# Gate and up of a fused FNet and ReGLU layer: one pass over all tokens with 33 block products in place of two passes with 18

## The chip, the cores and the metric

The kernel runs on 1 core of a Trainium2 chip. The metric is the device time of one execution in microseconds (us), the median of several runs; smaller is better. The core has five engines that work side by side and wait for each other by semaphores: PE (matmul, into the PSUM memory), DVE (elementwise), ACT (elementwise and functions), POOL or GpSimd (elementwise here, and issue of transfers), and SP (issue of transfers). SBUF is the memory on the chip from which they work. An engine takes its instructions in order.

## The reference

```python
xn = layernorm(x)                                   # x: 1 x 2048 x 640
a, b = xn @ hid_re.T, xn @ hid_im.T                 # 640 x 640
y = seq_re @ a - seq_im @ b                         # 2048 x 2048
gate, up = xn @ W_gate, xn @ W_up                   # 640 x 1728
h = gate * (gate > 0) * up
out = x + y + h @ W_down                            # 1728 x 640
```

All in float32. The 2048 tokens and 640 features are the sizes that set the work; 1728 is 13 times 128 plus 64.

## The kernel before

Float32 accuracy is had by splitting each operand into a high part in the rounded format fp32r and a low part that is the rest. One *product* is a 128x128 weight block by a 128x512 token block, and `mm3` makes it of three matmuls (high by high, high by low, low by high), L139 to L141. To split, ACT writes the high part (`copy`, L130, or the first line of `split`, L133) and DVE subtracts it (L134, L875).

The work runs in three stages.

**Stage one** normalizes the tokens and applies the sequence transform. It streams the transform matrices (`raw`, `tk`) in, splits them into a ring of buffers (`cb`) and multiplies by the tokens (`xs_early`, `xs_late`). It goes chunk by chunk of 512 columns; a scheduler sets the order of its instructions from the order in which `drive(4, 2)` starts units. The results are added on DVE to `sa` and `sb` and stored to DRAM as `pq` (L667). Beside it, `token_sets` makes sums and differences of token blocks for the second stage, on DVE, and stores them to DRAM (`sets`).

**Stage two, gate and up,** covers 398.2 to 730.4 us. A weight tile of 128 columns of gate and of up holds 10 blocks of 128x128. The tokens are taken in two halves `q` of 1024, and the loop `gate_up(n)` runs 26 units: 13 weight tiles for each half. In a unit, a 2x2 block scheme with fewer products (sums `S1` to `S4` of weights and `T1` to `T4` of tokens) makes 18 products in place of 20. So a weight tile costs 36 products. `Weights` loads a tile (640 KB) for each unit, makes its sums on DVE (`sums`, L861 to L865) and splits them. Partial results are copied from PSUM by ACT (`p`, `u`, L130) and added on DVE (L945, L963); `finals` makes relu(gate) times up (L888) and POOL stores 512 KB of `hd` (L889). The 64 leftover columns of gate and up go through `gate_up_rest`, 10 products for each half, at the start and at the end of the stage; their weights are `wr`. Also in this stage, `pair_weights` and `quad_weights` prepare sums of the last stage's weights (`pw`) and store them in DRAM (`wparts`, `wquads`), and `grow` adds up parts of `hd` and `pq` by transfers (`grown`).

The order in stage two is written by hand: PE, DVE and ACT (`PINNED`) take their instructions as the Python code calls them; the order of SP's and POOL's transfers is left to the scheduler.

**Stage three, the last stage,** from 730.4 us, multiplies hidden rows by the down weights and the hidden transform. It loads token rows (`rw`, from `pq` and `hd`) and weights (`wt`, from `wparts`) through SP, splits the rows into `cb` and multiplies. Its order comes from `drive_last`, which starts after named instructions of stage two (`issue_after`). Its first unit, the *lead*, was prepared in stage two by `lead_load` and `lead_split`; its 18 matmuls stand between the last product of stage two and the others of stage three.

```python
        for f in urgent[n]:
            f()
        copy(p1, b1)
        if ahead:
            ahead.high(0)
        block(b2, A12, B21, True, False)
        block4(b2, A4, 0, True)
        tt(oa[:, c0], b2, p1, op=OP.add)
        if n > 0:
            the_rest()
        if n + 2 < NU:
            weights[n + 2] = Weights(n + 2)
```

## Time and profile before

| what | value |
|---|---|
| median of 3 runs | 1023.11 us (1022.81 to 1023.18) |
| span of the profiled execution, first to last instruction | 1021.1 us |
| instructions in it | 12761 |
| HBM read and written | 203.26 and 72.89 MB |
| busy share of the span: PE, weight loads, DVE, ACT, POOL | 99, 82, 81, 45, 11% |
| gate and up in the trace | 398.2 to 730.4 us |

The time of the profiled execution itself is known by its span only. In the views, an instruction is named by its engine, its line in the kernel, what it writes and what it reads (`out<-in`), with the tile's partitions and elements. A group's row gives the busy time of all, the mean duration of one in ns, and the idle time of the engine just ahead of them with what ended it. A row of the timeline gives the start and the duration in us, then the instruction, then in brackets the idle time before and its releaser. A row of a window gives its length and the busy time of each engine. "PE 99%" in the chain of work means that, followed back from the last instruction, 99% of the span was PE's own.

### The profile page before, as it was taken

How to read it: one execution, taken by the hardware profiler on the slowest of the kernel's cores; microseconds unless marked ns; L12 is line 12 of the kernel's file. 1: busy time of each engine (PE TensorE's matmuls, PEld its weight loads, DVE VectorE, ACT ScalarE, POOL GpSimd, SP SyncE). 2: the span in 40 equal slices, each digit the busy share in tenths (PEclk: the TensorE clock that was granted, in tenths of full speed). 3: DMA queues.
4: the chain of work that ended last, by engine and by line, in shares of the span. 5: the costliest groups of instructions: out<-in, count | busy, mean ns of one | idle time of the engine just before them, and what ended most of it. 6: DMA issues, size and time to landing. Idle time of an engine off the chain costs nothing.

```text
span 1021.1 us, 12761 instructions
## 1 busy us (share of the span) xinstructions
PE 1015.6 (99%) x4510; PEld 840.8 (82%) x4510; DVE 823.5 (81%) x1162; ACT 454.9 (45%) x588; POOL 117.2 (11%) x189
## 2 busy tenths in 40 slices
PE   9999999999999999999999999999999999999998
PEld 7888888888888888888888888888888888888887
DVE  7967976969979697688888977787597888589887
ACT  6664453333334444434445444443443454454552
POOL 2000010121110001321111111111100000000001
PEclk9999999999999999999999999999999999999999
DMA  9884744976869666874658989899798879999784
GB/s 336 314 270 173 265 149 142 330 259 200 348 210 340 222 190 224 261 232 167 232 208 286 285 295 316 289 341 313 234 335 250 256 249 325 328 326 315 219 284 165
DMA packets 113872, 267.57 MB, mean 262 GB/s; under 512 B 13104, under 2 KB 58096, under 8 KB 112176
## 3 DMA queue, kind: packets, MB, share of 16 engines
q1 hardware_dynamic: 92416, 179.03, 52.5%
q0 software_dynamic: 20960, 87.31, 24.6%
q8 instruction: 35, 0.57, 0.2%
q10 hardware_dynamic: 432, 0.43, 0.1%
q14 instruction: 29, 0.24, 0.1%
HBM read 203.26 MB, written 72.89 MB: 270 GB/s over the span
## 4 chain that ended last, share of the span: by engine, by line
PE 99%; DMA 0%; ACT 0%; DVE 0%; SPq 0%; issue 0%
PE ps L140 32%; PE ps L139 32%; PE ps L141 32%; PE ps L527 3%; PE ps L556 1%; PE ps L1368 1%; DMA raw<-in_dft 0%; ACT cb L357 0%; ACT xs_early L258 0%; DVE y L1225 0%; SPq L596 0%; ACT mv L234 0%
## 5 line engine op out<-in xcount | busy, mean ns | idle before, releaser
L139 PE MATMUL ps<-cb,wt 128*128 128x512 f32 (+1 forms) x407 | 157.9, 388 | 0.0
L141 PE MATMUL ps<-cb,wt 128*128 128x512 f32 (+1 forms) x407 | 157.9, 388 | 0.0
L140 PE MATMUL ps<-cb,wt 128*128 128x512 f32 (+1 forms) x407 | 157.9, 388 | 0.0
L133 ACT ACTIVATE cb<-rw 128x1024 fp32r<-128x1024 f32 (+1 forms) x94 | 89.2, 960 | 77.1 <-PE ps L141 56.5
L134 DVE TENSOR_TENSOR cb<-rw,cb 128x1024 fp32r<-128x1024 f32 (+1 forms) x94 | 102.6, 1101 | 22.3 <-ACT cb L133 21.7
L133 ACT ACTIVATE cb<-raw 128x1024 fp32r<-128x1024 f32 x64 | 67.9, 1061 | 105.2 <-PE ps L141 97.0
L134 DVE TENSOR_TENSOR cb<-raw,cb 128x1024 fp32r<-128x1024 f32 x64 | 78.2, 1222 | 31.5 <-ACT cb L133 31.3
L141 PE MATMUL ps<-xs_early,gw 128*128 128x512 f32 x260 | 101.2, 389 | 0.0
L139 PE MATMUL ps<-xs_early,gw 128*128 128x512 f32 x260 | 101.2, 389 | 0.0
L140 PE MATMUL ps<-xs_early,gw 128*128 128x512 f32 x260 | 101.1, 389 | 0.0
L139 PE MATMUL ps<-cb,xs_late 128*128 128x512 f32 x232 | 90.2, 389 | 0.0
L140 PE MATMUL ps<-cb,xs_late 128*128 128x512 f32 x232 | 90.2, 389 | 0.0
L141 PE MATMUL ps<-cb,xs_late 128*128 128x512 f32 x232 | 90.2, 389 | 0.0
L139 PEld LDWEIGHTS ps<-cb,wt 128*128 128x128 f32 x407 | 76.4, 188 | 16.0 <-DVE y L1225 0.2
L141 PEld LDWEIGHTS ps<-cb,wt 128*128 128x128 f32 x407 | 76.4, 188 | 15.7
L140 PEld LDWEIGHTS ps<-cb,wt 128*128 128x128 f32 x407 | 76.4, 188 | 15.6
L139 PE MATMUL ps<-cb,xs_early 128*128 128x512 f32 x226 | 87.9, 389 | 0.0
L140 PE MATMUL ps<-cb,xs_early 128*128 128x512 f32 x226 | 87.9, 389 | 0.0
L141 PE MATMUL ps<-cb,xs_early 128*128 128x512 f32 x226 | 87.9, 389 | 0.0
L130 ACT ACTIVATE gw<-z 128x1024 fp32r<-128x1024 f32 (+1 forms) x52 | 56.4, 1110 | 38.6 <-PE ps L141 23.6
L130 ACT ACTIVATE u<-ps 128x512 f32<-128x512 f32 x52 | 31.1, 598 | 89.6 <-PE ps L141 77.7
L875 DVE TENSOR_TENSOR gw<-z,gw 128x1024 fp32r<-128x1024 f32 (+1 forms) x52 | 64.8, 1284 | 1.9 <-ACT gw L130 1.8
(209 smaller groups left out, 1989.4 us busy)
## 6 DMA issues: line engine op xcount, KB each, us to landing
raw<-in_dft SPq DMA_DIRECT2D x94, 512.0 KB, 5.4
wt<-wparts SPq DMA_DIRECT2D x74, 256.0 KB, 4.3
wparts<-pw POOLq DMA_DIRECT2D x12, 1408.0 KB, 7.9
z<-in_wgu SPq DMA_DIRECT2D x26, 640.0 KB, 5.6
rw<-hd SPq DMA_DIRECT2D x27, 512.0 KB, 6.2
hd<-ob POOLq DMA_DIRECT2D x26, 512.0 KB, 4.8
wt<-wparts SPq DMA_DIRECT2D x29, 384.0 KB, 5.4
rw<-pq SPq DMA_DIRECT2D x19, 512.0 KB, 6.4
```

The lines of the kernel that those rows point to most:

```text
L130: return nc.scalar.activation(o, i, AF.Copy)
L133: nc.scalar.activation(hi, src, AF.Copy)
L134: return nc.vector.tensor_tensor(lo, src, hi.bitcast(F32), op=OP.subtract)
L139: nc.tensor.matmul(ps, wh, mh, start=first, stop=False, skip_group_check=more)
L140: nc.tensor.matmul(ps, wh, ml, start=False, stop=False, skip_group_check=more)
L141: nc.tensor.matmul(ps, wl, mh, start=False, stop=last, skip_group_check=more)
L527: nc.tensor.matmul(E[0, key], xn_part(n * SG + j, d)[v == 1], b[:, int(v == 2), j], start=False, stop=n % NH == NH - 1 and (j, v) == (SG - ...
L556: nc.tensor.matmul(E[c, key], xn_part(j, d)[v == 1], b[c][0][:, int(v == 2), j], start=j == 0 and v == 0, stop=False)
L875: tt(self.w[:, 1, cs], self.z[:, cs], self.w[:, 0, cs].bitcast(F32), op=OP.subtract)
L1368: nc.tensor.matmul(B[out], w[:, v, oo : oo + P], b, start=False, stop=last and v == 1, skip_group_check=more)
```

## The change

Gate and up now goes once over all 2048 tokens. The 5 blocks of each weight (gate and up) and 4 chunks of 512 tokens form a 2x5 by 5x4 block product that is made by 33 products for a weight tile in place of 36. Each product takes a weight operand (raw or one of 23 sums) and a token operand (raw or one of 28 sums and differences). The results share partial sums that live in PSUM:

- `seed` copies a bank of PSUM to another, with a sign, and the next products add to it (ACT, L940); `snap` copies a bank to SBUF (`ev`, ACT, L175); `add` adds a snap into a bank, `addout` and `both` make sums, `final` makes relu(gate) times up (DVE, L950 to L967). A weight tile has 8 seeds, 9 snaps, 4 adds, 7 addouts, 1 both and 4 finals.
- Tables give each step of a weight tile a key, in units of one product. The steps of neighbouring tiles lie 33 keys apart and overlap; all events of the stage are sorted by key, and PE, DVE and ACT take them in that order.
- Weights are loaded once (13 times 640 KB). Their sums are made by GpSimd, 23 of 128x128 a tile (L907), and split by ACT and DVE in pieces (`w3` of 3 blocks, `w1`, `wa`, `wb`).
- The token sums are made by GpSimd in stage one, in 4 slices of 128 columns a chunk (`token_slice`, 10 operations of 128x512 and 41 of 128x128 each), and kept in DRAM (`tok`). 18 raw blocks are loaded and split at the end of stage one; the 28 sums are loaded and split in stage two, 14 of them into the pool `mv` and 14 into slots of `xs_early` and `r1` that come free.
- The leftover columns' 20 products stand at the start: 10 ahead of the first tile, 10 in the gaps of the first tile. The lead's 6 products stand in the gaps of the last tile.
- Results are stored by SP, 52 times 256 KB (L970). The preparation for the last stage comes as 29 tasks (24 `pair_half`, 5 quads) at even distances; all of `grown` is made in stage two.

By the two orders, PE has 4377 matmuls after and 4494 before, and POOL has 221 transfers after and 166 before.

```diff
-        def sums(self):
-            a21, z = self.z2[:, : 2 * P], self.z
-            zz = lambda b: z[:, b : b + 2 * P]
-            tt(zz(S1), a21, zz(A22), op=OP.add)
-            tt(zz(S2), zz(S1), zz(A11), op=OP.subtract)
...
+STEPS = (
+    (0.0, 'mm', 11, 0, 0, 20, 'new', -1), (1.59, 'seed', 16, 11, -1, ()), (3.0, 'mm', 16, 0, 1, 21, '', -1),
+    (4.0, 'mm', 13, 0, 2, 18, '', 11), (5.59, 'seed', 19, 13, 1, ()), (6.5, 'seed', 20, 16, 1, ()),
...
+    (46.6, 'both', 7, 10, 25, -1, 1, ()), (48.0, 'mm', 7, 6, 1, 44, '', -1), (49.59, 'addout', 7, 17, '-', (7,)),
...
+    (62.0, 'mm', 3, 7, 0, 47, '', 10), (64.44, 'addout', 3, 9, '-', (3,)), (65.6, 'final', 3, 7, ()),
+)
...
+        def sums(part):
+            for o, op, a, b in part:
+                pin(tt(at(o), at(a), at(b), op=OP.add if op == "+" else OP.subtract))
...
+    for n, b in (("mv", UPPER), ("prep", 2), ("w3", 5), ("w1", 3), ("wa", 2), ("wb", 2), ("ev", 11)):
...
+    def sum_step(n, o, op, a, b):
+        nc.gpsimd.tensor_tensor(operand(n, o), operand(n, a), operand(n, b), op=OP.add if op == "+" else OP.subtract)
...
+    def seed(n, x, s, sign, done):
+        banks[n, x] = new_bank()
+        nc.scalar.activation(banks[n, x], banks[n, s], AF.Copy, scale=float(sign))
+        release(n, done)
...
+    def add_snap(n, x, s, op, done):
+        b = banks[n, x]
+        tt(b, b, snaps[n, s], op=OP.add if op == "+" else OP.subtract)
+        release(n, done)
...
+        held["dve"] = nc.vector.scalar_tensor_tensor(t, i0, 0.0, i1, op0=OP.max, op1=OP.mult)
+        release(n, done)
+        cs = slice(g % 2 * CH, (g % 2 + 1) * CH)
+        nc.sync.dma_start(hd[g // 2][TILES[n]][:, cs], t)
...
+    for i, o in enumerate(combos[:UPPER]):
+        at(-59, load_upper, o)
+        at(-5 + 1.35 * i, split_slot, o)
...
+    for i, (load, prepare, rounded, store) in enumerate(tasks):
+        key = first_task + (last_task - first_task) * i / (len(tasks) - 1)
+        at(key - 14, load)
+        at(key, prepare)
+        at(key + SPLIT_AHEAD, rounded)
+        at(key + SPLIT_AHEAD + 2, store)
...
+    for i in range(3):
+        for j in range(SG):
+            at(END + (36, 37, 40, 41, 44, 45)[2 * i + j] + 0.3, lead_multiply, i, j)
+
+    events.sort(key=lambda e: e[:2])
     with tc.manual_schedule(engines=PINNED):
-        third[0]()
...
+        for key, _, f in events:
             f()
```

The first place is ACT's row at the start of gate and up, in the new program. `w3` and `w1` are rounded weights, `mv` token sums, `ev` copies out of PSUM, `ps` to `ps` is a seed; the brackets name the queues and engines waited for (DMASW: transfers issued by POOL, DMAHW: by SP).

```order
L178 ACTIVATE pw_3328<-st_3326 128x640
L175 ACTIVATE w3_3381<-gw_3359 128x384 [waits DMASW4_49,DMASW5_49,DMASW3_49,DMASW6_49,DMASW2_49,DMASW7_49,DVE_49,Pool_49]
L175 ACTIVATE w1_3386<-gw_3359 128x128
L178 ACTIVATE mv_3331<-mv_3331 128x512 [waits DMAHW4_49,PE_49,Activation_49]
L1002 ACTIVATE ev_3415<-ps_3316 64x512 [waits PE_49]
L178 ACTIVATE mv_3333<-mv_3333 128x512 [waits DMAHW5_49]
L175 ACTIVATE w3_3429<-gw_3359 128x384 [waits Pool_49]
L178 ACTIVATE mv_3335<-mv_3335 128x512 [waits DMAHW6_49]
L178 ACTIVATE mv_3337<-mv_3337 128x512 [waits DMAHW7_49]
L793 ACTIVATE mv_3339<-mv_3339 128x512 [waits DMAHW0_49]
L1002 ACTIVATE ev_3456<-ps_3317 64x512 [waits PE_49]
L940 ACTIVATE ps_3320<-ps_3318 128x512 [waits PE_49]
```

Before, the weights were rounded into buffers of their own; now the first `w3` waits for six queues of POOL, the last of them that of the last store of `sa`, since the memory of `w3` held `sa` and `sb`. The third seed follows 9 rows further on.

The second place is SP's row at the hand-over to the last stage. Before (L855 is the load of the last unit's weights, `rw` and `wt` belong to the last stage):

```order
L855 DMA z_5477<-in_wgu 128x1280 [waits DMAHW7_49,DVE_49]
L1289 DMA wt_5805<-wparts_94 128x2x384 [waits DMAHW0_49,PE_49]
L1261 DMA rw_5807<-pq2_88 128x1024 [waits DMAHW1_49,DMASW3_49,DVE_49]
L1261 DMA rw_5809<-pq2_88 128x1024 [waits DMAHW2_49,DVE_49]
L1289 DMA wt_5811<-wparts_94 128x384 [waits DMAHW3_49]
```

After (L970 are the stores of finals; the last four of them are shown):

```order
L970 DMA hd1_90<-ev_6570 128x512 [waits DMAHW5_49,DVE_49]
L1308 DMA wt_6738<-wparts_93 128x2x384 [waits DMAHW6_49,PE_49]
L970 DMA hd0_89<-ev_6646 128x512 [waits DMAHW7_49,DVE_49]
L970 DMA hd0_89<-ev_6586 128x512 [waits DMAHW0_49,DVE_49]
L1280 DMA rw_6740<-pq2_87 128x1024 [waits DMAHW1_49]
L970 DMA hd1_90<-ev_6681 128x512 [waits DMAHW2_49,DVE_49]
L1280 DMA rw_6742<-pq2_87 128x1024 [waits DMAHW3_49]
```

The loads of the last stage stood behind a weight load of stage two, and now stand behind and between stores that wait for DVE's last finals.

The third place is PE's row there, in the new program: the end of gate and up and the first product of the last stage.

```order
L186 MATMUL ps_3316<-mv_6485,mv_6487 128x512
L184 MATMUL ps_3319<-xs_early_75,wb_6503 128x512 [waits Activation_49]
...
L184 MATMUL ps_3318<-xs_early_75,w3_6606 128x512 [waits DVE_49]
...
L186 MATMUL ps_3320<-r1_2858,wb_6503 128x512
L184 MATMUL ps_3322<-r1_2858,w1_6351 128x512
L185 MATMUL ps_3322<-r1_2858,w1_6351 128x512
L186 MATMUL ps_3322<-r1_2858,w1_6351 128x512
L184 MATMUL ps_3321<-cb_6752,wt_6738 128x512 [waits Activation_49]
L185 MATMUL ps_3321<-cb_6752,wt_6738 128x512 [waits DVE_49]
```

The lead products (`mv_6485` by `mv_6487`) now stand ahead of the last five products of gate and up, and the last stage's `cb` follows these directly; before, the 18 lead matmuls stood in between.

663 lines of the change are left out of this document (309 added, 354 removed), and 32 rows, old and new, of tables (STEPS, SUMS, TOKEN_SUMS, WEIGHTS).

## The prediction

> **What bounds the kernel now.** I read the page's shares and its chain of work first.
>
> ```profile
> span 1021.1 us, 12761 instructions
> ...
> PE 1015.6 (99%) x4510; PEld 840.8 (82%) x4510; DVE 823.5 (81%) x1162; ACT 454.9 (45%) x588; POOL 117.2 (11%) x189
> ...
> PEclk9999999999999999999999999999999999999999
> ...
> PE 99%; DMA 0%; ACT 0%; DVE 0%; SPq 0%; issue 0%
> ```
>
> TensorE (PE) is busy 99% of the span, it is 99% of the chain, and its granted clock reads 9 in each slice. No wait of another engine sets the end, so the span is the number of matmuls times their spacing. Next come the windows of gate and up (405.0 to 723.4, its 26 units) and of one chunk of the sequence transform (columns: busy time of PE, weight loads, DVE, ACT, POOL; clock; DMA share; GB/s).
>
> ```profile
> 405.00:723.40 318.40, 318.40 (x1406) 263.55 (x1405) 252.99 (x438) 137.76 (x185) 57.71 (x92) 1.00 0.81 270
> 202.00:268.00 66.00, 66.00 (x293) 54.66 (x292) 55.13 (x64) 22.45 (x22) 11.59 (x17) 1.00 0.76 273
> ```
>
> PE has no idle time in either. A matmul costs 318.40/1406 = 0.2265 us, a product of three 0.680 us. DVE is 79% busy in gate and up, ACT 43%.
>
> **What the change removes.** 13 weight tiles lose 3 of 36 products: 13 × 3 × 3 = 117 matmuls, 117 × 0.2265 = **26.5 us**. The 20 products of the 64 leftover columns and the 6 lead products stay and only move. Since PE is the bound with nothing beside it, all 26.5 us would be gained if PE stayed fed. The sum below is therefore 26.5 us less the new stalls of PE.
>
> **Can the others keep up in one tile's 33 products (33 × 0.680 = 22.4 us)?** The rows for the prices:
>
> ```profile
> L963 DVE TENSOR_TENSOR oa<-ps,u 128x512 f32<-128x512 f32 x26 | 17.9, 690 | 34.6 <-PE ps L141 34.6
> L862 DVE TENSOR_TENSOR z<-z 128x256 f32<-128x256 f32 x26 | 11.1, 425 | 0.9
> L865 DVE TENSOR_TENSOR z<-z 128x128 f32<-128x128 f32 x26 | 7.4, 284 | 0.0
> L133 ACT ACTIVATE cb<-raw 128x1024 fp32r<-128x1024 f32 x64 | 67.9, 1061 | 105.2 <-PE ps L141 97.0 <-issue 5.0 <-DVE st L447 1.7
> L130 ACT ACTIVATE u<-ps 128x512 f32<-128x512 f32 x52 | 31.1, 598 | 89.6 <-PE ps L141 77.7 <-DVE sets_b L440 5.5 <-DVE sets_b L421 5.5
> L360 POOL TENSOR_TENSOR cb<-raw,cb 128x512 fp32r<-128x512 f32 x3 | 3.8, 1289 | 0.0
> ...
> 7.44 0.19 POOL L364 TENSOR_TENSOR mv<-stat,cb 128x1 f32<-128x1 f32 x1 [6.99 <-DVE cb L360]
> ...
> 610.20 0.69 DVE L963 TENSOR_TENSOR oa<-ps,u 128x512 f32<-128x512 f32 x1 [1.73 <-PE ps L141]
> 610.81 0.41 DVE L1050 TENSOR_TENSOR pw<-pw 128x256 f32<-128x256 f32 x1
> ```
>
> The last two rows show that a DVE instruction starts 0.08 us before its forerunner's recorded end, so a 128x512 takes 0.61 us of DVE. DVE has 16 such steps on PSUM in a tile (4 add, 7 addout, 1 both, 4 final): 9.8 us. The low halves of the weights are 8 of 128x384 (about 0.48 us of DVE, between the rows of 256 and 512 columns less the same 0.08), one of 512 and one of 128 columns (0.61 and 0.20): 4.6 us. Preparing the last stage's weights adds 29 tasks over 13 tiles, each four 128x128 sums and a low half, 1.3 us: 2.9 us a tile. That makes 17.3 us of 22.4, 77%, as now. ACT has 8 seeds and 9 snaps (0.598 us recorded, 0.52 with the same overlap): 8.8 us, some 4 us of high halves and 1 us of preparation: 14 us, 62%. GpSimd has 23 sums of 128x128, which no row shows: bounds 0.19 us (one column) and 1.29 us (512 columns); on the line between them 0.46 us, 10.7 us a tile, 48%. At the upper bound 23 × 1.29 = 29.7 us would exceed the tile, and GpSimd would be the bound; I take 0.46 since the one-column row shows the fixed part. DVE writing PSUM and ACT copying PSUM to PSUM have no row either: 0.60 to 0.69 us is what the same sizes cost from PSUM to SBUF, and I use that; if PSUM output cost the 128x1024 row's 1.06 us, ACT's 8 seeds would add 3.7 us a tile and still fit. So nothing is over 100%; what is lost, is lost to lateness at single places.
>
> **Place 1, the start of gate and up.** Now:
>
> ```profile
> 398.40 0.39 PE L139 MATMUL ps<-xs_early,wr 128*128 128x512 f32 x1
> ...
> 398.99 0.68 DVE L566 TENSOR_TENSOR sa<-ps,sa 128x512 f32<-128x512 f32 x1
> ...
> 400.07 0.53 POOL L667 DMA_DIRECT2D pq<-sa  x1 [7.54 <-DVE z L861]
> 404.60 1.09 POOL L417 DMA_DIRECT2D sets_b<-rows  x2 [4.00 <-DMA pq<-sa]
> ```
>
> The last sums of the transform are stored at 400.07 and their memory is free at 404.60. In the new order ACT's first weight rounding (w3) waits for that very store, and in ACT's row stand 19 more activations behind it up to the third seed. The 10 leftover products last from 398.4 to 405.2. After 404.6 ACT does w3, w1 and the first token split (0.48 + 0.25 + 0.52 us, the first two estimated on the line between ACT's rows), so the first product starts at 405.9 instead of 405.2, and it waits for DVE's low half of the token block, 0.4 us more. The first seed is ACT's eighth after that, ready near 405.9 + 8 × 0.52 = 410.1; its product has three products ahead of it and could start at 408.3: 1.8 us. By the same count the next two seeds come 0.9 and 0.3 us late, and the one behind them about 1. That is 5 us in the first 12 products. To product 60 DVE has 28 token splits beside the tile work (17.3 − 2.9 = 14.4 us a tile, 26.2 in 60 products): 28 × 0.61 + 26.2 = 43.3 us in 60 × 0.68 = 40.8 us, 2.5 us more. Value **7.5 us**; bounds 0 (if memory is free and the loads are early) and 12.
>
> **Place 2, the hand-over to the last stage.** Now:
>
> ```profile
> 713.23 1.26 SPq L1289 DMA_DIRECT2D wt<-wparts  x1
> 714.53 0.47 SPq L1263 DMA_DIRECT2D rw<-hd  x1
> ...
> 731.27 0.36 SPq L1263 DMA_DIRECT2D rw<-hd  x1
> ...
> 731.04 2.52 ACT L133 ACTIVATE cb<-rw 128x1024 fp32r<-128x1024 f32 x3
> ...
> 732.12 2.96 DVE L134 TENSOR_TENSOR cb<-rw,cb 128x1024 fp32r<-128x1024 f32 x3 [0.27 <-ACT cb L133]
> ...
> rw<-pq SPq DMA_DIRECT2D x19, 512.0 KB, 6.4
> ...
> st<-pq SPq DMA_DIRECT2D x1, 512.0 KB, 3.6
> ...
> L134 DVE TENSOR_TENSOR cb<-raw,cb 128x1024 fp32r<-128x1024 f32 x64 | 78.2, 1222 | 31.5 <-ACT cb L133 31.3
> ```
>
> The last stage's raw blocks are issued on SP before 715.11, and 18 lead matmuls (4.1 us) run while they are rounded from 731.0 on. In the new order the stores of the results stand on SP, and the first raw block (rw) stands behind the stores of finals 0 and 1 of the last tile. These finals wait for the last products: after PE's last product DVE still has addout 4, final 0 and final 1, some 1.5 us, SP's waiting stores take 0.5 us more, so rw is issued 2 us after PE's last product, lands 3.6 to 6.4 us later, is rounded by ACT (1.06 us) and, before the second matmul, by DVE (1.22 us). The lead products have by then gone into the gaps of the last tile and cover nothing. PE waits 2 + 3.6 + 2.3 = 8 to 2 + 6.4 + 2.3 = 11 us. Value **9 us**; bounds 0 (issued as early as now) and 11. A place further on is not late again: the loads behind are issued within 2 us.
>
> **Between them.** The tables leave little room at three places of a tile: the sum `both 7` is asked for at 13.6 products and needed by a product at 15 (0.95 us, for a 0.69 us step); add 23 to seed 1 to its product, 0.3 us spare; seed 16, 0.4 us. One of 29 preparation tasks (four 128x128 sums, over 1 us in one burst) comes every 12 products; I take one in two to strike such a place, some 12 to 14 strikes of 0.4 us: **5 us**, bounds 0 and 10. PE is in order, so each is lost.
>
> **What costs nothing.**
>
> ```profile
> z<-in_wgu SPq DMA_DIRECT2D x26, 640.0 KB, 5.6
> ```
>
> Token sums on GpSimd in the first stage: 4 slices of 41 × 0.46 + 10 × 1.29 = 32 us, 127 us in a first stage of 398 us, beside a busy PE; if they are late, tokens come late and place 1 grows. DVE loses its token work there, which gains nothing while PE is full. The weights are loaded 13 times 640 KB in place of 26, the stores carry the same bytes, and the DMA share was 0.81 with PE full; so I take nothing for transfers, and what a late queue costs stands under D.
>
> **The sum.** −26.5 + 7.5 + 5 + 9 = −5.0 us against the profiled 1021.1: 1016.1. The median of the runs is 1023.11, 2.0 us above the span, so **1018.1 us**. With the bounds of the three places (0 to 33 us) and 26.5 off: 996.6 to 1029.6.
>
> **Rivals.** (B) The cover is better: loads and rounding are early, hand-over 3, start 3, between 1 us. Time 1023.1 − 26.5 + 7 = 1003.6. For it: ACT's and DVE's shares leave a quarter free. Against it: the orders of both places, as told.
> (C) Slower: DVE and GpSimd get in each other's way at SBUF. Rows that bear on it:
>
> ```profile
> 7.59 1.29 POOL L360 TENSOR_TENSOR cb<-raw,cb 128x512 fp32r<-128x512 f32 x1
> ...
> 4.87 0.42 DVE L251 TENSOR_SCALAR r<-r,mv 128x384 f32<-128x384 f32 x1
> ...
> 8.43 0.66 DVE L251 TENSOR_SCALAR r<-r,mv 128x384 f32<-128x384 f32 x1
> ```
>
> The same DVE operation takes 0.42 us with GpSimd idle and 0.66 us when it starts inside a GpSimd sum (7.59 to 8.88). Some 24 DVE steps of each tile read SBUF with both inputs (weight lows, finals, preparation, and split lows), 312 in all, and a GpSimd sum runs for 48% of the time. If each that meets one waits 0.23 us, half a sum, that is 312 × 0.48 × 0.23 = 34 us of DVE, and GpSimd waits as long. DVE would rise from 77% to near 90% of a tile; with the narrow places I take half to reach PE, 17 us, from 12 to 25 with a first stage that suffers too. Time 1018 + 18 = 1036, 1030 to 1043. It decides from about 5 us of lost PE time on. Against it: the first stage's DVE has slack, and a late step costs nothing outside the three narrow places.
> The Trainium skill, "SBUF — State Buffer", section "Who interferes with whom", says that DVE and GpSimd share a port pair as an exclusive lock, held for a whole instruction, and that a DVE instruction with two SBUF inputs competes for it with a GpSimd one that reads SBUF. The stretch from 0.42 to 0.66 us agrees in kind; no DVE row with two SBUF inputs meets a GpSimd sum in this trace, so the rule stays open here. By it the sum would be 1036, without it 1018.
> (D) GpSimd's queue is late as a whole: its sums, the preparation's stores and the growing of hd stand in one row, and a sum that waits holds all behind it. A weight sum late by a quarter of a tile (5.6 us) in half of the tiles costs 36 us: 1054. For it: one in-order queue with 299 sums and 221 DMAs (166 before). Against it: 48%, and sums asked for 10 to 40 products ahead.
> That the change does not do what it says I leave out: the new program's PE row has 117 matmuls fewer.
>
> **Chances.** Forecast (1009 to 1025) 0.40; B (997 to 1009) 0.17; C 0.33; D 0.10. A measurement of this kernel can tell 0.2%, 2 us, from no change. Faster than 1021.1: B and three quarters of the forecast, 0.47; within 2 us the rest of the forecast and the edge of C, 0.15; slower the rest of C and D, 0.38. The range from 1003 to 1042 leaves out some 0.08 below and 0.12 above; the likeliest case's own range is 1009 to 1025.
>
> **What would show it.** 117 fewer matmuls. A gap of PE near 405 to 412, ACT's w3 released by the store of sa; a gap of 8 to 11 us at the hand-over, released by rw<-pq, ACT and DVE; short gaps in each tile released by DVE or ACT; no gap in the first stage. DVE near 77% and POOL near 48% in gate and up. For C: w3 lows well above 0.56 us and 128x128 sums of POOL above 0.46. I am wrong if the gaps of PE in gate and up differ from 21.5 us by more than 10, above all if the hand-over's gap is missing, or if POOL's 128x128 sum is far from 0.46 us.

## The result, and the profile after

The changed kernel takes 1248.65 us (median of 4 runs, 1246.92 to 1250.3); the kernel before took 1023.14 us in the same rounds. The ratio is 1.220, interval 1.2185 to 1.222: the change makes the kernel 22% slower. The forecast was 1018.1 us, range 1003 to 1042; the result lies outside it and on the other side.

The page of the changed kernel, with the rows that answer to those of before (busy shares, the granted clock in 40 slices, the chain):

```profile
span 1247.3 us, 13677 instructions
...
PE 1044.9 (84%) x4393; PEld 841.1 (67%) x4393; DVE 873.9 (70%) x1210; ACT 522.8 (42%) x828; POOL 532.5 (43%) x741
...
PEclk9998997985897997989999878989998999999999
...
PE 35%; POOL 21%; issue 15%; DMA 14%; DVE 10%; ACT 4%; SPq 1%; DVEq 0%; POOLq 0%; ACTq 0%
```

PE has 117 matmuls fewer, as announced, and is no longer the chain: 99% has become 35%, and POOL, idle time put down as "issue" and transfers make up half. The clock, 9 in every slice before, falls to 5 and 7 in some. The stages, cut at the first leftover product and at the first product of `cb` by `wt` behind the lead (columns as before: stretch, length, PE, weight loads, DVE, ACT, POOL, clock, DMA share, GB/s). The kernel before:

```profile
0.00:398.40 398.40, 396.64 (x1775) 328.41 (x1776) 326.44 (x434) 178.31 (x226) 44.10 (x72) 1.00 0.71 249
398.40:734.40 336.00, 336.00 (x1483) 278.13 (x1482) 267.83 (x459) 148.16 (x198) 61.36 (x97) 1.00 0.79 263
734.40:1021.10 286.70, 282.98 (x1254) 234.27 (x1252) 229.21 (x271) 128.48 (x164) 11.79 (x20) 1.00 0.85 279
```

The changed kernel:

```profile
0.00:542.30 542.30, 418.42 (x1776) 337.06 (x1777) 350.03 (x407) 176.92 (x235) 315.73 (x370) 0.89 0.62 214
542.30:956.70 414.40, 340.23 (x1367) 267.84 (x1365) 290.23 (x529) 211.66 (x421) 208.05 (x356) 0.92 0.47 150
956.70:1247.30 290.60, 286.28 (x1253) 236.21 (x1253) 233.68 (x275) 134.18 (x172) 8.72 (x16) 0.99 0.83 279
```

Stage one, where no product was changed, grows by 143.9 us; gate and up by 78.4 in spite of the 26.5 saved; the last stage by 3.9. The sum is the 226.2 us between the spans. By kind: PE's idle time grows from 5.5 to 202.4 us, and PE's busy time by 29.3 with 26.5 us of matmuls fewer, so the lower clock costs some 56 us. No engine is near full in gate and up (DVE 290 of 414): this is waiting, not work.

**Stage one.** The waits of the changed kernel up to 542.3 us (engine, what it starts, what released it; total, times, longest):

```profile
ACT sb L175 <- DMA pq<-sb: 107.0, 4, 41.9
...
PE ps L184 <- ACT sb L175: 89.8, 4, 36.9
POOL tok L469 <- issue: 39.9, 14, 7.6
POOL r L455 <- issue: 36.7, 12, 8.3
POOL r L453 <- issue: 25.2, 7, 5.5
```

ACT waits four times for a store of `sb`, PE for ACT. The store is an instruction in POOL's row, and that row holds the token sums. POOL's timeline around the second of these waits, a sum group and then the transfers behind it:

```profile
245.33 13.57 POOL L464 TENSOR_TENSOR r<-r 128x128 f32<-128x128 f32 x13
...
280.70 0.79 POOL L455 DMA_DIRECT2D r<-in_xt  x1 [1.35 <-issue]
281.51 0.47 POOL L464 TENSOR_TENSOR r<-r 128x128 f32<-128x128 f32 x1
284.11 0.78 POOL L455 DMA_DIRECT2D r<-in_xt  x1 [2.13 <-issue]
287.61 0.98 POOL L469 DMA_DIRECT2D tok<-r  x1 [2.73 <-issue]
291.23 0.79 POOL L453 DMA_DIRECT2D r<-rows  x1 [2.65 <-issue]
...
299.99 0.60 POOL L690 DMA_DIRECT2D pq<-sb  x1
```

And ACT's, which has nothing between these two rows:

```profile
262.14 1.06 ACT L178 ACTIVATE cb<-raw 128x1024 fp32r<-128x1024 f32 x1 [3.02 <-PE ps L186]
305.07 1.08 ACT L175 ACTIVATE sb<-ps 128x512 f32<-128x512 f32 x2 [41.87 <-DMA pq<-sb]
```

The chain reads: the store of `sb` is issued at 299.99, behind the slice's sums and transfers; ACT, in order, stands at the copy into `sb` for 41.87 us; the `cb` roundings behind that copy wait too, and PE runs out of `cb`. Two prices are visible. The sums come at 13.57/13 = 1.04 us, not 0.46; while DVE, too, has run out of work, one takes 0.47 (281.51). And the next transfer of `tok`, `rows` or `in_xt` does not follow the last at once: the four that start at 280.70, 284.11, 287.61 and 291.23 lie 3.4 to 3.6 us apart. A sum starts directly behind such a transfer (281.51), so the row stands still only for what no sum fills, put down as "issue": 101.8 us in stage one by the three rows of waits. Two of POOL's groups over the whole run:

```profile
L464 POOL TENSOR_TENSOR r<-r 128x128 f32<-128x128 f32 x164 | 141.7, 886 | 3.0
...
L469 POOL DMA_DIRECT2D tok<-r x28 | 27.6, 985 | 40.7 <-issue 39.9 <-POOL r L464 0.8
```

**Gate and up.** Its waits, of the engines:

```profile
ACT pw L1090 <- DVE pw L1088: 50.4, 18, 10.2
PE ps L184 <- ACT ps L940: 50.2, 20, 7.8
...
ACT ps L940 <- DVE ps L950: 39.7, 13, 9.3
DVE ev L955 <- DMA hd<-ev: 38.4, 11, 7.1
...
ACT w L175 <- DMA pq<-sa: 20.3, 1, 20.3
```

And of SP's queue:

```profile
SPq L1078 <- DMA wparts<-pw: 115.0, 24, 11.1
SPq L970 <- DVE ev L967: 103.3, 28, 13.6
```

Once in nearly every tile PE waits for a seed. The seed (seed 1) waits for DVE's add 23; in DVE's row ahead of that stands addout 5, which waits for an `ev` buffer that a store of `hd` has not yet emptied. In four of the eleven waits (21.8 of the 38.4 us) DVE came before SP had issued that store: it stood behind loads for the preparation (L1078), and each of these waits until POOL has stored the buffer's former content to `wparts`. (Ahead of two of the four SP also stood some 6 us at a weight load, L901, for POOL's weight sums.) In the other seven (16.5 us) the store was on its way; the slowest, issued at 723.21, took 7.85 us to land. A second way goes through ACT: ahead of the seed in its row can stand its rounding for a preparation task (L1090), which waits for DVE's sums of `pw`, and these stand behind the same addout (at 734.95 ACT has waited 10.19 us so). So four in-order rows hang on one another: POOL, SP, DVE, ACT.

**The clock after a gap.** At the hand-over PE stops for 9 us. Windows of the 8 us behind it:

```profile
956.70:959.00 2.30, 1.83 (x4) 1.14 (x5) 1.66 (x2) 0.82 (x2) 0.00 (x0) 0.50 1.06 406
...
961.00:963.00 2.00, 2.00 (x6) 1.52 (x6) 1.46 (x2) 1.87 (x4) 0.00 (x0) 0.50 1.06 394
963.00:965.00 2.00, 2.00 (x10) 1.65 (x9) 2.00 (x4) 1.04 (x2) 0.00 (x0) 0.97 1.06 399
```

For 6 us the granted clock is 0.50 and only 4 to 6 matmuls run in 2 us; then it is back. This gap costs its own length and about 3 us more.

### The profile page after: what moved, and what is told of

It is laid out like the page before. It is cut to its first block, busy times and chain, and to the rows that moved or that the text cites. A ratio compares the mean times of both kernels' runs of the same rounds, so it can differ in the third digit from the quotient of the medians.

```text
span 1247.3 us, 13677 instructions
## 1 busy us (share of the span) xinstructions
PE 1044.9 (84%) x4393; PEld 841.1 (67%) x4393; DVE 873.9 (70%) x1210; ACT 522.8 (42%) x828; POOL 532.5 (43%) x741
## 4 chain that ended last, share of the span: by engine, by line
PE 35%; POOL 21%; issue 15%; DMA 14%; DVE 10%; ACT 4%; SPq 1%; DVEq 0%; POOLq 0%; ACTq 0%
PE ps L184 12%; PE ps L185 11%; PE ps L186 11%; POOL r L464 11%; DMA hd<-ev 3%; POOL r L460 2%; POOL r L459 2%; DMA raw<-in_dft 2%; POOL tok L469 2%; DMA wt<-wparts 2%; DMA wparts<-pw 2%; DMA pq<-sa 2%; POOL gw L907 2%; DVE ev L955 2%; DMA pq<-sb 1%
## 5 line engine op out<-in xcount | busy, mean ns | idle before, releaser
L464 POOL TENSOR_TENSOR r<-r 128x128 f32<-128x128 f32 x164 | 141.7, 886 | 3.0
L1256 POOL DMA_DIRECT2D out<-y x16 | 8.7, 545 | 308.1 <-DVE y L1244 307.5
L907 POOL TENSOR_TENSOR gw<-gw 128x128 f32<-128x128 f32 x203 | 118.9, 615 | 31.5 <-DVE w L921 25.6
L179 DVE TENSOR_TENSOR cb<-tk,cb 128x1024 fp32r<-128x1024 f32 x32 | 49.5, 1548 | 115.3 <-ACT cb L178 115.2
L179 DVE TENSOR_TENSOR cb<-raw,cb 128x1024 fp32r<-128x1024 f32 x64 | 86.2, 1347 | 39.0 <-ACT cb L178 39.0
L955 DVE TENSOR_TENSOR ev<-ps,ev 128x512 f32<-128x512 f32 x91 | 62.5, 687 | 64.9 <-DMA hd<-ev 38.4
L184 PE MATMUL ps<-cb,xs_late 128*128 128x512 f32 x232 | 93.3, 402 | 14.8 <-ACT sa L175 10.4
L184 PE MATMUL ps<-cb,gw 128*128 128x512 f32 x64 | 29.2, 456 | 89.8 <-ACT sb L175 89.8
L185 PE MATMUL ps<-cb,xs_late 128*128 128x512 f32 x232 | 93.8, 404 | 7.9 <-DVE cb L179 7.8
L184 PEld LDWEIGHTS ps<-cb,wt 128*128 128x128 f32 x407 | 77.1, 189 | 25.4 <-ACT cb L178 9.4
L186 PE MATMUL ps<-cb,xs_late 128*128 128x512 f32 x232 | 92.3, 398 | 0.0
L940 ACT ACTIVATE ps<-ps 128x512 f32<-128x512 f32 x104 | 59.4, 581 | 77.4 <-DVE ps L950 39.7
L185 PEld LDWEIGHTS ps<-cb,wt 128*128 128x128 f32 x407 | 77.1, 189 | 17.4 <-DVE cb L179 1.5
```

The lines of the kernel that those rows point to most:

```text
L179: return nc.vector.tensor_tensor(lo, src, hi.bitcast(F32), op=OP.subtract)
L184: nc.tensor.matmul(ps, wh, mh, start=first, stop=False, skip_group_check=more)
L185: nc.tensor.matmul(ps, wh, ml, start=False, stop=False, skip_group_check=more)
L186: nc.tensor.matmul(ps, wl, mh, start=False, stop=last, skip_group_check=more)
L464: pin(tt(at(o), at(a), at(b), op=OP.add if op == "+" else OP.subtract))
L907: nc.gpsimd.tensor_tensor(operand(n, o), operand(n, a), operand(n, b), op=OP.add if op == "+" else OP.subtract)
```

## The experiments

Each time is of a single run, beside one of the kernel before, which took 1022.85 to 1023.22 us. Differences under about 2 us are not read. In the last stage all variants of the changed kernel take 290 to 292 us, so each is told by its stage one (542.3 in the changed kernel) and its gate and up (414.4).

### Stage one: sums, transfers or stores in POOL's row

Three parts were taken out of POOL's row, each alone.

```diff
 # tok_on_dve (token_slice)
-        tt = nc.gpsimd.tensor_tensor
+        tt = nc.vector.tensor_tensor
 # tok_dma_sp (token_slice, the three transfers)
-                nc.gpsimd.dma_start(by_chunk(at(k * NT, NT)), by_chunk(xt[k * P : (k + 1) * P])[:, :, cs])
+                nc.sync.dma_start(by_chunk(at(k * NT, NT)), by_chunk(xt[k * P : (k + 1) * P])[:, :, cs])
...
 # stores_on_sp (the stores of sa and sb; those of first and its load likewise)
-        store = lambda m, at, t: defer(1, lambda: nc.gpsimd.dma_start(pqd[c][m][:, at : at + t.shape[1]], t))
+        store = lambda m, at, t: defer(1, lambda: nc.sync.dma_start(pqd[c][m][:, at : at + t.shape[1]], t))
```

> The token sums of stage one run on DVE in place of GpSimd; nothing else is changed. Every theory that blames GpSimd for stage one expects the first leftover product near 400 to 410 us (542.3 in the changed kernel, 398.4 before) and a span near 1247 - 140 = 1107 us. If DVE becomes the bound of stage one instead (57 us of token work more on an engine that was 83% busy there before, less the token work that it had then), stage one ends at 430 or later. Gate and up keeps its 405 us from the first leftover product to its last product.

> The stores of sa and sb (pq, first) and the load of first are issued by SP in place of POOL; the token sums stay on GpSimd. Queue theory (the stores stand behind token sums in POOL's row, ACT waits for the buffer of sb and stops rounding): ACT's wait for pq<-sb (107 us) goes, the first leftover product comes at 400 to 430 us, span 1105 to 1140. Port theory (GpSimd makes DVE's steps 0.26 us longer and DVE starves PE by itself): the first leftover product stays beyond 490 us and the span above 1195.

> The token slices' own transfers (loads of rows and in_xt, stores to tok, 56 in all) are issued by SP; the sums stay on GpSimd, the stores of sa and sb on POOL. In the changed kernel each of these transfers holds POOL's row for some 3.6 us (1.0 us and an idle time of 2.65 us that no view explains), near 50 us of the 95 us of a slice. If that is what makes the slices late, POOL's waits labelled issue go, a slice takes some 55 us, the first leftover product comes at 400 to 440 us (542.3 in the changed kernel) and ACT's wait for pq<-sb falls from 107 to below 25 us. If the long sums (0.83 to 0.89 us) are the cause by themselves, the first leftover product stays beyond 480 us.

| kernel | time | stage one | gate and up |
|---|---|---|---|
| changed kernel, profiled execution | span 1247.3 | 542.3 | 414.4 |
| tok_on_dve | 1192.87 | 488.5 | 411.8 |
| stores_on_sp | 1204.34 | 502.6 | 407.9 |
| tok_dma_sp | 1199.1 | 497.5 | 408.9 |

Each takes 40 to 54 us off, none brings stage one back to 398. With the sums on DVE the transfers still stand in POOL's row, one issue every 3.7 to 4.0 us and nothing between them:

```profile
162.64 0.99 POOL L469 DMA_DIRECT2D tok<-r  x1 [4.75 <-issue]
166.63 1.01 POOL L469 DMA_DIRECT2D tok<-r  x1 [3.01 <-issue]
170.30 0.79 POOL L453 DMA_DIRECT2D r<-rows  x1 [2.66 <-issue]
```

and DVE, in order, now waits for the last of them (row of its waits: `DVE r L459 <- DMA r<-rows`, 52.6 us in 3 waits). With the stores on SP the wait for `pq<-sb` is gone, but the four slices still begin some 92 us apart on POOL, and the last comes late at the end of the stage:

```profile
ACT r L178 <- DMA r<-tok: 86.6, 7, 74.1
```

With the transfers on SP, the idle time labelled "issue" is gone from POOL's waits, but SP stands 131.7 us at its `tok` stores for POOL's sums, and its row now delays the loads of the transform matrices (waits `DVE raw L717 <- DMA raw<-in_dft` 52.9 us in 6). By its time alone each run lies where its expectation had put the other theory (beyond 430, 490 and 480 us). The waits tell more: DVE is 76% busy in tok_on_dve and so not its bound, and each run has a late in-order row. So all three theories of one culprit fell: each part alone makes a row late, and moving it makes another row late. Then two parts were moved together, with two edits of gate and up (below):

```diff
 # dve_sp_act12: tok_on_dve + tok_dma_sp, and
-    for n, b in (("mv", UPPER), ("prep", 2), ("w3", 5), ("w1", 3), ("wa", 2), ("wb", 2), ("ev", 11)):
+    for n, b in (("mv", UPPER), ("prep", 2), ("w3", 5), ("w1", 3), ("wa", 2), ("wb", 2), ("ev", 12)):
...
-        nc.sync.dma_start(hd[g // 2][TILES[n]][:, cs], t)
+        held[n, g] = lambda: nc.scalar.dma_start(hd[g // 2][TILES[n]][:, cs], t)
...
+            if what == "final":
+                at(k0 + key + 2.5, lambda n, g: held[n, g](), n, args[0])
```

> Token sums on DVE, their transfers on SP, finals stored by ACT, 12 copy buffers. Stage one: with the transfers off POOL, DVE's wait for r<-rows (52.6 us in the run with the sums on DVE) goes and the first leftover product comes at 400 to 420 us; if SP's row (raw loads in order behind token stores) takes the place of POOL's, raw loads are late and it comes beyond 440. Gate and up: as with finals on ACT, less some 15 us for the twelfth buffer: 350 to 385 us in place of 414.4. Span 1040 to 1100.

1090.56 us. Its windows of stage one and of gate and up:

```profile
0.00:421.80 421.80, 405.62 (x1776) 332.22 (x1777) 371.39 (x611) 178.36 (x235) 70.61 (x119) 0.98 0.81 275
421.80:798.50 376.70, 327.43 (x1367) 256.04 (x1365) 298.19 (x529) 212.62 (x421) 201.91 (x347) 0.97 0.50 163
```

Stage one falls by 120.5 us, more than the 53.8 and 44.8 of the two moves alone together. The two edits of gate and up, each alone, change stage one by 1.3 us. So 120.5 of the 143.9 us came from token sums and their transfers in POOL's row. The other 23.4 stay. DVE is 88% busy there, 45 us more than in the kernel before, and PE's largest wait is for DVE's `cb` (9.5 us); that the sums' time on DVE is all of the 23.4 no run shows.

### Does GpSimd relieve DVE?

From that kernel, the normalizing steps of the slices, 40 of 128x512, went back to GpSimd (and the preparation's loads five keys later):

```diff
-            pin(tt(x, x, at(WORK_MR, NT), op=OP.add))
-            pin(tt(x, x, at(WORK_MR + NT, NT), op=OP.mult))
+            pin(nc.gpsimd.tensor_tensor(x, x, at(WORK_MR, NT), op=OP.add))
+            pin(nc.gpsimd.tensor_tensor(x, x, at(WORK_MR + NT, NT), op=OP.mult))
...
-        at(key - 14, load)
+        at(key - 9, load)
```

> As the run with token sums on DVE, their transfers on SP, finals on ACT and 12 copy buffers (1088.7 us), but the 40 steps of 128x512 that normalize the tokens go back to GpSimd (27 us of DVE less), and the loads of the preparation are asked for 9 in place of 14 products ahead. If DVE is what holds stage one at 421.8 us there (88% busy), the first leftover product comes at 403 to 412; if GpSimd's lock on DVE costs what the steps cost, it stays at 418 to 430. Gate and up stays within 15 us of 376.7.

1114.45 us. Stage one is 15 us longer, beyond both ranges:

```profile
0.00:437.00 437.00, 407.90 (x1776) 332.37 (x1777) 383.19 (x571) 177.96 (x235) 142.58 (x150) 0.98 0.78 266
```

DVE lost 40 steps, 40 × 0.69 = 27.5 us, and is busy 11.8 us *longer*. The 571 steps left grew by 39.3 us, that is 0.98 us for each step that GpSimd took: giving work away cost DVE more than doing it. Gate and up is longer too, 385.9 us in place of 376.7; whether the later loads did that, no run tells.

The same was tried in the kernel before, alone: 12 GpSimd sums of 128x128 beside each of 25 units, of data that is there anyway, with no reader.

```diff
+    def extra(w):
+        for i in range(12 if w else 0):
+            o = S1 + i % 8 * P
+            nc.gpsimd.tensor_tensor(spare_t, w.z[:, o : o + P], w.z[:, o : o + P], op=OP.add)
...
+        extra(ahead)
```

> The kernel before, with 300 GpSimd sums of 128x128 more in gate and up (12 in each of 25 units, of the next unit's weight sums, into a tile that nobody reads). No other instruction waits for them, so this is the price of the sums beside DVE by itself. Port theory: DVE steps with two SBUF inputs that meet a sum last 0.26 us longer (gw<-z,gw 1.22 to 1.48 or more), a sum takes 0.46 us alone and 0.8 to 1.0 beside DVE; DVE's busy time in gate and up rises from 265 to 295 to 335 us, and since PE has DVE's slack of 20% the time rises by 0 to 20 us, to 1023 to 1043. Without contention DVE's rows stay within 0.03 us of the old ones and the time within 2 us of 1023.

1034.88 us against 1022.96. Its window of gate and up, and three of its groups:

```profile
398.40:746.50 348.10, 339.58 (x1486) 277.73 (x1485) 305.76 (x460) 147.79 (x198) 248.82 (x397) 1.00 0.77 255
```

```profile
L914 POOL TENSOR_TENSOR spare<-z 128x128 f32<-128x128 f32 x300 | 189.3, 631 | 22.6 <-DVE z L862 2.0
...
L951 DVE TENSOR_TENSOR oa<-ps,p 128x512 f32<-128x512 f32 x26 | 18.0, 691 | 4.4 <-PE ps L142 1.0 <-DVE ob L889 0.5
...
L864 DVE TENSOR_TENSOR z<-z 128x256 f32<-128x256 f32 x26 | 15.8, 608 | 0.0
```

DVE's work rises from 267.8 to 305.8 us, 0.127 us for each of the 300 sums, and gate and up grows by 12.1 us, 8.5 of them idle time of PE, which had none. The steps with both inputs in SBUF are stretched (128x256 from 418 to 608 ns); those that read PSUM are not (691 ns). The Trainium skill, "SBUF — State Buffer", section "Who interferes with whom", has it that DVE and GpSimd share one pair of ports, and that a DVE instruction with two SBUF inputs contends there while one with at most one, outside its two-port modes, does not. Here the trace agrees, and adds the price.

### Gate and up: which row is late?

Four edits of the changed kernel, each alone: weight sums only for the first tile; one more `ev` buffer; the stores of finals on ACT instead of SP (as in the diff above); no preparation.

```diff
 # sums_once
-        for key, *what in SUMS:
+        for key, *what in SUMS if n == 0 else ():
 # ev12: the "ev" line above; hd_on_act: the "held" lines above
 # after_no_prep (with raw weights copied to wparts and wquads)
-    for i, (load, prepare, rounded, store) in enumerate(tasks):
+    for i, (load, prepare, rounded, store) in enumerate(tasks[:0]):
```

> The weight sums of GpSimd are made for the first tile alone; tiles 2 to 13 use the first tile's sums, so their results are not the reference's. POOL's row loses 276 sums. Port theory for gate and up (sums slow DVE by 0.26 us where both meet, and come late): gate and up shrinks from 405 us to below 360 and its regular stall at r,wa goes. Ring theory (DVE waits for a copy buffer ev whose store has not landed): the stall at r,wa stays above 30 of its 46 us and gate and up shrinks by less than 25 us. Stage one stays as it is, so the span is 1220 to 1240 by the ring theory, below 1200 by the port theory.

> The pool of copies ev has 12 buffers in place of 11. Ring theory: DVE's wait for hd<-ev (38.4 us, once in each tile) falls below 10 us, PE's stalls at r,wa from 46 to below 15, and with the slow clock behind each stall gate and up shrinks by 40 to 70 us; span 1180 to 1207. If SP's late issue is what counts (the stores stand behind loads that wait for wparts), the wait moves to the next buffer and gate and up shrinks by less than 20 us.

> The stores of finals (hd) are issued by ACT, 2.5 products behind the final, in place of SP; nothing else is changed. If the stores are late because SP stands at loads of pw that wait for wparts (SP: 115 us of such waits), DVE's wait for hd<-ev falls from 38.4 to below 15 us and gate and up, from the first leftover product to the first product of the last stage (414.4 us), shrinks by 25 us or more. If the landing itself is late (2.7 us median, 7.8 at most, beside the transfers of grown), the wait stays above 25 us and gate and up shrinks by less than 15. The first raw block of the last stage no longer stands behind finals, so the gap of 9.0 us at the hand-over falls to 5 or less.

> The changed kernel with only the preparation left out (raw weights copied to wparts and wquads by POOL; the last stage's results are not the reference's). If the preparation holds up the finals' stores through SP's row (115 us of waits for wparts there) and so the copy buffers, gate and up falls from 414.4 to 350 to 375 us and DVE's wait for hd<-ev from 38 to below 12. If the ring of 11 buffers is short by itself, it stays above 385.

| kernel | time | gate and up | DVE's wait `ev <- hd<-ev` |
|---|---|---|---|
| changed kernel | span 1247.3 | 414.4 | 38.4 |
| sums_once | 1239.13 | 404.5 | 40.3 |
| ev12 | 1232.87 | 399.3 | 17.8 |
| hd_on_act | 1235.25 | 402.5 | 22.2 |
| after_no_prep | 1219.95 | 339.4 | 11.3 |

Without the weight sums gate and up is only 10 us shorter, and DVE's wait stays: POOL's sums and the port are not the main cause. A larger ring and an earlier store give 15 and 12 us, less than the 40 to 70 and the 25 expected: they shorten the wait at the end of the chain and leave its start. What stays of the wait in hd_on_act are stores that ACT had issued before DVE came and that had not landed (the one of 718.61 took 5.9 us), so the theory of the late landing has a part in it. The gap at the hand-over, 5 or less by the expectation, is 6.31 us. Without the preparation 75.0 us go, and the stores of finals land in 2.0 us (median) in place of 2.7. The window and the two rows of waits of that kernel:

```profile
587.60:927.00 339.40, 316.32 (x1366) 256.73 (x1364) 239.53 (x379) 199.35 (x392) 162.62 (x303) 0.98 0.38 116
```

```profile
PE ps L184 <- ACT ps L940: 5.0, 4, 2.0
...
DVE ev L955 <- DMA hd<-ev: 11.3, 12, 1.6
```

PE's wait for seeds falls from 50.2 to 5.0 us, and the clock rises from 0.92 to 0.98. (Its stage one is longer, 587.6 us, since the copies of the raw weights are issued in POOL's row there.) The same two removals were made from dve_sp_act12:

> As the run with token sums on DVE, their transfers on SP, finals on ACT and 12 copy buffers (1088.7 us; gate and up 376.7 us), but the 29 preparation tasks are left out; POOL copies raw weights to wparts and wquads instead, so the last stage's results are not the reference's. If the preparation's two buffers (loads that wait for stores, in SP's, DVE's and ACT's rows) and its DVE time make the stalls, gate and up comes to 330 to 345 us, and its waits for seeds from 32 to below 15. If the step table itself is too tight, it stays above 360.

> As the run before, and the GpSimd weight sums are made for the first tile alone. With GpSimd out of gate and up, the port theory expects 5 to 15 us less than without the preparation alone; without contention it is the same within 3 us. What is left above 309 us of matmuls is then the table's own, the start and the hand-over.

1078.14 and 1073.3 us; gate and up 337.3 and 335.4. The window of the second:

```profile
445.40:780.80 335.40, 316.14 (x1366) 256.85 (x1364) 225.28 (x380) 199.74 (x392) 17.25 (x27) 0.98 0.37 115
```

Taking the weight sums away as well gives 2 us, no more than such a run can tell: once the preparation is gone, GpSimd's sums in gate and up cost about nothing. PE's 19 us of idle time lie in the first 60 us and at the hand-over (6.5), half a microsecond in the tiles between. Without the preparation the tables hold.

Together these runs part what the preparation costs. In dve_sp_act12, with twelve buffers and the stores on ACT, DVE's wait for `hd<-ev` is 0.5 us in all, and gate and up is 37.7 us shorter than in the changed kernel (the moves of stage one in it had changed gate and up by 2.6 and 5.5 us, each alone). Yet no_prep is another 39.4 us shorter. So the ring of copies carries some 30 to 38 of 77 us, and the rest of the preparation's cost comes another way.

### Mending the preparation

From dve_sp_act12 (376.7 in gate and up), or from norm_gpsimd (385.9) for the first:

```diff
 # sp_by_hand, from norm_gpsimd
-PINNED = {mybir.EngineType.PE, mybir.EngineType.DVE, mybir.EngineType.Activation}
+PINNED = {mybir.EngineType.PE, mybir.EngineType.DVE, mybir.EngineType.Activation, mybir.EngineType.SP}
 # prep_spread: ACT's rounding apart from DVE's sums
-        at(key + SPLIT_AHEAD, rounded)
-        at(key + SPLIT_AHEAD + 2, store)
+        at(key + 5, high)
+        at(key + 7, rounded)
+        at(key + 8, store)
 # lead_behind, on prep_spread
-            at(END + (36, 37, 40, 41, 44, 45)[2 * i + j] + 0.3, lead_multiply, i, j)
+            at(END + 70 + 2 * i + j, lead_multiply, i, j)
 # prep_store_act: the three stores to wparts and wquads
-            nc.gpsimd.dma_start(wquads[:, i], t["s"].rearrange("p s v n -> p s (v n)"))
+            nc.scalar.dma_start(wquads[:, i], t["s"].rearrange("p s v n -> p s (v n)"))
```

> As the run before, with SP's transfers of gate and up in the order of the keys too. The stall of 11.0 us in that stage (a load of pw that stood behind others in SP's row) goes and gate and up comes to 340 to 360 us; if waits for wparts still hold SP in order, it stays at 370 or more. Span 1040 to 1075.

> As the run with token sums on DVE, their transfers on SP, finals on ACT and 12 copy buffers (1088.7 us), but in each preparation task ACT's rounding stands 5 products behind DVE's sums and the low half 7 behind, in place of 0 and 1.5. There ACT, in order, waits 48.5 us for DVE's sums of pw, and the seeds stand behind it. If these waits make the seeds late, ACT's wait for pw falls below 20 us, PE's wait for seeds from 32.3 to below 20, and gate and up from 376.7 to 350 to 365 us. If the seeds are late by DVE's adds and the products themselves, gate and up stays above 370. Stage one stays within 8 us of 421.8.

> As the run before it, with the 6 lead products behind the last product of gate and up (as in the kernel before) in place of the gaps of the last tile. If the lead covers the wait for the first raw block, the gap ahead of the first product of the last stage falls by their 4.1 us, from some 6 to 2 us, and the last tile loses less than that by its open gaps: the first product of the last stage comes 1 to 4 us earlier than in the run before it. If the open gaps cost as much, it comes within 1 us of it.

> As the run with token sums on DVE, their transfers on SP, finals on ACT and 12 copy buffers (1088.7 us; gate and up 376.7 us), but the preparation's stores (wparts, wquads) are issued by ACT in place of POOL. If a buffer of the preparation comes free late because its store stands behind weight sums in POOL's row, SP's wait for wparts falls from 160 to below 80 us, DVE's and ACT's waits for pw fall and gate and up comes to 337 to 355 us, near the 337.3 us without any preparation. If it is DVE's time for the sums of pw that counts, gate and up stays above 365.

| kernel | time | gate and up |
|---|---|---|
| sp_by_hand | 1123.54 | 395.3 |
| prep_spread | 1107.72 | 396.1 |
| lead_behind | 1103.79 | 393.5 |
| prep_store_act | 1072.97 | 360.1 |

Two are misses the wrong way. An order of SP by the keys does not help, since SP still waits for `wparts` (150.8 us). Spreading a task took ACT's wait for DVE's sums of `pw` from 48.5 to 8 us, as expected, but PE's wait for seeds rose from 32.3 to 35.1: the task now holds its buffer longer, and the next task's load comes later (wait `DVE pw L1088 <- DMA pw<-in_hid` 35.8 us). The lead's products put back behind gate and up shorten the hand-over's gap from 6.3 to 3.5 us and give 2.6. Moving the preparation's stores out of POOL's row gives 16.6 us, between what the two theories asked for; SP's wait for `wparts` falls from 159.9 to 121.5 us only, PE's wait for seeds from 32.3 to 16.0, and 23 us above the 337.3 without preparation stay.

prep_store_act is the fastest variant that leaves nothing out, and it is 50.1 us slower than the kernel before (stage one +22.4, gate and up +24.1, last stage +3.6). No version that beats the kernel before was found.

## Why the prediction was wrong

**The saving and the floor: right.** 117 matmuls went. The 1365 of gate and up at 0.2266 us are 309.3 us, and the runs without preparation come within some 30 us of it.

**"What costs nothing": this step failed, by 144 us.** The prediction gave the token sums on GpSimd 32 us a slice "beside a busy PE" and saw only late tokens as a price. The slices begin some 95 us apart. Three terms were wrong or missing. A sum costs 0.89 us on the mean of stage one and 1.04 in the group beside a working DVE, not 0.46; 0.46 itself is right where DVE is out of the way (0.45 in the row at 546.28 below). The slices' 56 transfers were not counted at all: 49 us of issue and 101.8 us of still time between them in POOL's row. And the stores of `sa` and `sb` share the row, so POOL's lateness reached ACT, `cb` and PE. The first stage was taken as safe because its engines had slack; it was not asked what else is queued behind the new work. tok_on_dve, tok_dma_sp and stores_on_sp show each part, dve_sp_act12 that the first two together make up 120.5 us.

**"Between them", 5 us: failed.** PE's idle time in gate and up is 74.2 us, of which 16 are the start and the hand-over, so some 58 stand here, and most of 31 us of slow clock with them. The step named DVE's burst of a preparation task as the striker and the tables' narrow places as the struck. Without the preparation the tables do not stall, so the striker is right. But the blow is not DVE's 1.3 us alone, nor 0.4 us each time: the long waits behind it are for buffers. The preparation has two of them, whose loads wait on SP for stores that wait on POOL; the finals' stores stand behind these loads or land late, and the `ev` ring waits for those. after_no_prep shows the size (75.0 us with the clock), dve_sp_act12 that the ring is at most about half of it; prep_store_act, ev12 and hd_on_act each cut one link and get 12 to 17 us. How the rest divides between the preparation's buffers and its time on DVE stays open. On DVE too the preparation costs more than forecast: 290.2 − 239.5 = 50.7 us for 29 tasks, 1.75 each, not 1.3.

**The start, 7.5 us: mechanism right, size wrong.** ACT's first weight rounding waits for the store of `sa`, as told. POOL's row there in the changed kernel:

```profile
534.44 11.87 POOL L907 TENSOR_TENSOR gw<-gw 128x128 f32<-128x128 f32 x20
546.28 0.45 POOL L907 TENSOR_TENSOR gw<-st 128x128 f32<-128x128 f32 x1
...
547.24 0.53 POOL L690 DMA_DIRECT2D pq<-sa  x1
...
556.23 0.72 ACT L175 ACTIVATE w<-gw 128x384 fp32r<-128x384 f32 x2 [20.29 <-DMA pq<-sa]
557.53 0.80 PE L184 MATMUL ps<-mv,w 128*128 128x512 f32 x1 [6.91 <-ACT mv L178]
```

Weight sums stand ahead of that store, so it is issued 4.9 us behind the first leftover product, in place of 1.7 before. And it lands late, 8.9 us after its issue in place of 3.9: from 542.5 us on SP issues the loads of the token sums beside it, and the DMA share is 0.98 from 547 to 556 us, against 0.62 before (400 to 405). The prediction took nothing for transfers. The first product comes 15.2 us after the first leftover product, not 6.8; the prediction had 1.1 us for that rounding and its low half. It is 8.4. The other terms of the 7.5, seeds and splits that are late in the first tiles, come near: PE waits 4.5 us for ACT's seeds and DVE's adds between 557.53 and 600 us, against some 6.

**The hand-over, 9 us: right, step by step.** In the changed kernel:

```profile
949.55 0.49 SPq L1280 DMA_DIRECT2D rw<-pq  x1
955.58 1.06 ACT L178 ACTIVATE cb<-rw 128x1024 fp32r<-128x1024 f32 x1 [3.43 <-DMA rw<-pq]
956.69 0.80 PE L184 MATMUL ps<-cb,wt 128*128 128x512 f32 x1 [8.97 <-ACT cb L178]
957.95 0.80 PE L185 MATMUL ps<-cb,wt 128*128 128x512 f32 x1 [0.47 <-DVE cb L179]
```

PE's last matmul starts at 947.33, `rw` is issued about 2 us later, lands 6 us after that, and PE's gap is 8.97 and then 0.47 for DVE. Issue, landing, rounding and low half are the terms of the forecast.

**The clock: left out, 56 us.** The prediction priced a gap at its length. The gaps that end at 557.5, 698.8 and 956.7 us, 7 to 9 us long, are each followed by 4 to 6 us at half clock, with matmuls 0.43 us apart in place of 0.227. The Trainium skill, "TensorE: Matmul & The Clock Gate", "Part 1: The HAM clock gate (the "warmup" mystery)", says that the array falls to half its rate after an idle window of about 3.4 us and gives 426.7 ns from start to start at 512 columns; the trace agrees on the half rate (0.50) and on the spacing (0.427); the length of the window no run here measures. So even the forecast's own 9 us gap was worth 12.

**Rival C (the port): right rule, wrong weight.** It assumed 0.23 us for a DVE step that meets a sum; 0.127 us per sum and 0.26 for a step that meets one were measured (128x1024 in stage one: 1.22 us alone, 1.48 beside a sum). Its remark that no DVE row with two SBUF inputs meets a sum in the trace before is not quite so: one does, for 0.06 us (L639 at 13.24 us, not lengthened). In gate and up it matters little (2 to 10 us by no_prep_sums_once and sums_once). In stage one it doubles the sums' time on GpSimd. **Rival D (POOL's queue late as a whole): the right mechanism,** but with 36 us, a chance of 0.10, and placed in the weight sums of gate and up, which held SP's weight loads (L901) twice only, for 11.8 us.

**Why gate and up gains nothing even when it runs.** Without the preparation it takes 335 to 339 us against 336.0. The 26.5 us are eaten by the start, the hand-over and the slow clock behind both: 316.1 busy against 309.3, and 19 to 23 us idle.

## What to carry to other kernels

Before work is moved to an idle engine, list what else stands in its row, transfers and stores included, and follow who waits for each: an in-order row that is late is passed on to every engine whose buffers it frees. Price the moved work from a row where both engines run, not from one where the other rests; here GpSimd's sums doubled and DVE gained nothing. And a gap of PE of 7 to 9 us costs its length and about 3 us of slow clock more.

## What the runs showed of the hardware that was not expected

- Two transfers in 512-byte pieces that follow each other in POOL's row start at least 3.35 us apart, often 3.65: 0.8 to 1.0 us of issue and then some 2.6 us in which POOL does nothing ("issue"), against 0.5 to 0.6 us for a store of `sa` or `sb`. In stage one 33 of the 56 have a sum behind them, and each of these sums starts within 0.02 us. So sums between such transfers would fill the time; no run tried that order. What holds the next transfer back no view shows; it stays open.
- GpSimd's 128x128 float32 sum: 0.45 us alone, 0.63 us beside the DVE of gate and up in the kernel before, 0.89 us in stage one, 1.04 us in the group shown. DVE steps with both inputs in SBUF lengthen by 0.26 us where they meet one in full, whatever their own size; steps that read PSUM do not. Beside GpSimd's steps of 128x512 (1.29 us alone) it is 1.09 us (norm_gpsimd: 1.22 to 2.31), and in before_plus_sums, where a sum alone takes 0.40, it is 0.20. Each time that is the GpSimd step's own time less some 0.2 us.
- A 128x512 GpSimd step costs DVE 0.98 us, more than the 0.69 us of the step on DVE itself.
- Open: the 23 us in gate and up between prep_store_act (360.1) and no preparation (337.3). SP's wait for `wparts` is the largest there; no run took it away without the preparation.
